# Two interleaved transformer layers on one core: the first loads, the bound check and the query weights rearranged

## The chip, the cores and the metric

The kernel runs on one core of a Trainium2 chip. Its metric is the device time of one execution in microseconds (us), from five runs. Five engines work side by side: TensorE (PE, with its weight loads shown apart as PEld), VectorE (DVE), ScalarE (ACT), GpSimd (POOL), and SyncE (SP), which issues most DMAs. Each engine takes its instructions strictly in its own order, and a wait holds up all that is behind it on that engine.

## The reference

The input x has 2048 rows of 576 bf16 values. Two kinds of block alternate, A, B, A, B, each added to x after a layer norm without scale or shift.

Block A is linear attention with 32 heads of width 18 and a learned feature map:

```
q, k, v  = split(ln(x) @ wqkv)                  # per head, width 18
pq, pk   = q @ w_phi, k @ w_phi                 # 18 x 18 per head
phi_q    = [softmax(pq), softmax(-pq)]          # 36 features, phi_k the same from pk
kv, z    = sum over rows of phi_k^T v, of phi_k
o        = (phi_q kv) / (phi_q z + 1e-6)
x        = x + o @ wo
```

Block B is a bilinear gated unit: x + ((ln(x) @ w_gate) * (ln(x) @ w_up)) @ w_down, with 4608 inner columns. Both layers use the same weights.

## The kernel before, in words

**Tiles.** The 2048 rows are 16 tiles of 128 rows (NS), handled in 8 pairs (NB). The kernel fuses w_phi into the query and key weights once: for each of five blocks `kt` of 128 rows of wqkv (the last has 64 rows) it turns the raw block (`Wraw`) by five PE transposes into `WT`, copies that out of PSUM, and multiplies it by a block diagonal form of w_phi (`BDphi5`) in two half-groups of three matmuls, each followed by a cast into `Wk` or `Wq` (`t_fuse1`). So a half-group is 16 heads of one block.

**A program in two versions.** If the fused projections can't overflow, exp needs no maximum. A bound is computed on the chip: PE multiplies every raw block by itself (`t_flag`, "Gram" matmuls, 10 for a block), DVE takes the maxima, three fp32 matmuls turn the columns of maxima, and four small DVE operations make a flag. All engines load the flag and branch to the fast or the general version of all that follows. What is recorded up to the mark is common to both versions and is called the shared part here. With these inputs the fast version runs.

**Layer 1, block A, after the branch.** For each tile: layer norm (`t_ln`: statistics on DVE, the affine step `xln` on DVE or POOL, then a transpose into `xT`, by PE for the first two pairs and by DMA on SP's queue for the others), value projection (`t_v`), key projection and its four exps on ACT (`fast_front`), row sums on DVE (L1327), reciprocals on ACT or DVE, two products on POOL (L1342), and the kv matmuls (`kv_ops`). For one tile a projection is 18 matmuls that use half the PE's rows each, two at a time. Key and value tiles stay in two PSUM banks of sums (`kvb`) until all 16 tiles are done; `t_barrier` then masks them into `BD`. Query projections (`t_qproj`) may start once tile 8 is accumulated (`pqg`), and are stored in the place of `xT`.

**From BD to block B.** Tiles 0 and 1 go through a chain of their own (`t_aout`: numerator, denominators, transposes, Wo, layer norm), and then block B starts on the first pair (`t_bmain`, `gu_quad`, L1662). It also waits for `wloaded`: the loads of Wr, Wg and Wu (10 MB) stand on SP behind the DMA transposes of the last pair of layer 1's layer norm, because part of that space holds `Wraw` and `WT` before.

**What sets the order.** Nothing is ordered by hand. Each piece of work is a thread of requests, and a planner (`Sched.run`) picks the request that could start first by its own duration estimates, shifted by priorities, by an `age`, and by a table of offsets for each thread (`AGES`). The choice between engines (`alt`) is made there too. The planned order of each engine is then the program, so a change of an estimate or of `AGES` moves instructions everywhere. SP issues x tile 0, raw blocks 0 and 2, x tile 1, raw block 4 as two halves of 64 partitions, the value weights and x pairs 1 to 3; ACT's queue issues w_phi and raw blocks 1 and 3 (`t_load`).

Of the kernel before, what the change touches and what calls it, by code (L numbers as in the profile page):

```python
# [19 lines left out]
    "ain1_10": -143, "ain1_12": -228, "ain1_13": 255, "ain1_14": 386, "ain1_5": -137, "ain1_9": -364, "ain2_14": -581, "aout1_0": 157,  # L20
    "aout1_2": -123, "aout1_3": -52, "aout2_0": -253, "aout2_1": 5, "aout2_2": -160, "aout2_3": -342, "bar1": -1385, "bar2": -651, "bdphi": 141,
    "bepi0": 843, "bepi6": 1283, "bepi7": -480, "fusek0": 115, "fusek1": 188, "fusek3": 103, "init": 18, "k2_6": -644, "k2ln0": 204, "k2ln1": 1008,
    "kv2_6": 13, "kv2_7": -60, "lnA1_0a": 99, "lnA1_0b": 308, "lnA1_1": 24, "lnA1_4": -54, "lnB1_0a": -834, "lnB1_0b": -218, "lnB2_0a": -48,
    "lnB2_0b": 270, "pq1_11": 192, "pq1_2": -84, "pq1_5": 108, "pq1_6": 202, "pq1_7": 20, "pq1_8": 114, "pq1_9": 166, "pq2_11": 158, "pq2_12": -146,
    "pq2_13": -162, "pq2_14": -2, "pq2_15": -156, "pq2_2": 116, "pq2_3": -76, "pq2_5": -209, "pq2_6": -46, "pq2_7": -103, "pq2_8": 448, "pq2_9": 459,
    "v1_0": -129, "v1_13": 57, "v1_14": -38, "v1_3": -2, "v1_4": 70, "v1_6": -13, "v1_8": -25, "v1_9": -41, "v2_14": -73, "v2_15": -358,
# [268 lines left out]
class Sched:  # L295
# [110 lines left out]
    def run(self):  # L406
        tr = self.tr
        while True:
            progressed = False
            again = True  # L410
            while again:
                again = False
                for th in list(self.threads):
                    while th.req is not None and th.req[0] not in ("ops", "alt", "pe2", "dma", "acq", "acqn"):
# [18 lines left out]
                        elif kind == "mark":  # L433
                            tr.set_mark(r[1])
                            t_ = self.tr.fin[tr.lastw[r[1]]] + 500.0
# [113 lines left out]
            else:  # L549
# [4 lines left out]
                start = max(issue, self.dma_free["sp"], 1300.0)  # L554
                xfer = nbytes / self.dma_bw
                self.dma_free["sp"] = start + xfer
                sp_time = r[8] if len(r) > 8 else 480.0
                fin = max(start + xfer + self.dma_lat, issue + 2.1 * sp_time) + (1500.0 if sp_time > 1000 else 0.0)
# [23 lines left out]
def d_pe(n):  # L582
    return max(n, 64) / 2.4 + (7.0 if 288 <= n < 512 else 3.0)
# [10 lines left out]
def d_actc(n):  # L594
    return n / 1.2 + 50.0
# [29 lines left out]
class K:  # L625
    def __init__(self, nc, A_x, A_wqkv, A_w_phi, A_wo, B_w_gate, B_w_up, B_w_down, out, fast, base=None):
# [10 lines left out]
        self.vlead = 5  # L637
        self.row2 = True
        self.fage = 300.0
        self.fageq = 0.0  # L640
        self.fage2 = 300.0
# [4 lines left out]
        self.qlead = 8 if fast else 8  # L646
# [3 lines left out]
        self.lnlead = 8  # L650
# [4 lines left out]
        self.pqg = 8 if fast else 10  # L655
# [21 lines left out]
    def alloc(self):  # L677
# [10 lines left out]
        self.cst = A("cst", [128, 4], F32)  # L688
        self.flg = A("flg", [1, 8], F32)
# [46 lines left out]
    def lend(self):  # L736
# [56 lines left out]
        self.sm_of = {}  # L793
        self.wd_slot = {}
# [3 lines left out]
        self.g_out = g("out")  # L798
        self.g_et = [g("et%d" % i) for i in range(self.NET)]
# [16 lines left out]
    def t_init(self):  # L816
# [19 lines left out]
            Op(100, lambda e: e.memset(s.mask9[:], 1.0), writes=[("mask9",)]),  # L836
            Op(100, lambda e: e.memset(s.maskf[:], 1.0), writes=[("maskf", 0), ("maskf", 1)]),
# [45 lines left out]
    def t_flag(self):  # L883
# [5 lines left out]
        gots = yield ("acqn", ["pb"], 2)  # L889
        banks = [g_[1] for g_ in gots]  # L890
        for kt in range(5):
            yield ("wait", ("ld", "raw", kt))
            yield ("ops", "pe", [Op(55, (lambda e, m=m, c0=c0, kt=kt, bank=banks[m // 3], c=128 * (m % 3), st=(kt == 0 and c0 == 0 and m in (0, 3)): e.matmul(
                s.ps[:, bank, c:c + 128], s.Wraw[:, kt, c0 + 128 * m:c0 + 128 * m + 128], s.Wraw[:, kt, c0 + 128 * m:c0 + 128 * m + 128], start=st, stop=(kt == 4 and c0 > 0), skip_group_check=True)),
                reads=[("Wraw", kt)], writes=[("pbd", banks[m // 3])], excl=[("pb", banks[m // 3])]) for c0 in (0, D) for m in range(5)])
        yield ("ops", "dve", [Op(d_dve(n), (lambda e, c=c, bank=bank, n=n: e.tensor_reduce(s.cst[:, c:c + 1], s.ps[:, bank, 0:n], AX.X, ALU.max)),
                                 reads=[("pbd", bank)], writes=[("cst", c)], excl=[("pb", bank)]) for c, bank, n in ((1, banks[0], 384), (2, banks[1], 256))])
        for bank in banks:
            yield ("rel", "pb", bank)
        (_, bank), = yield ("acqn", ["pb"], 1)  # L900
        yield ("ops", "pe", [Op(150, (lambda e, c=c: e.matmul(s.ps[0:1, bank, 128 * c:128 * c + 128], s.cst[:, c:c + 1], s.identf[:], start=(c == 0), stop=(c == 2), skip_group_check=True)),
                                reads=[("cst", c), ("identf",)], writes=[("pbd", bank)], excl=[("pb", bank)]) for c in range(3)])
# [3 lines left out]
        yield ("ops", "dve", [  # L906
            Op(470, (lambda e: e.tensor_reduce(s.flg[0:1, 0:3], s.ps[0:1, bank, 0:384].rearrange("p (c n) -> p c n", c=3), AX.X, ALU.max)), reads=[("pbd", bank)], writes=[("flg", 0)], excl=[("pb", bank)]),
            Op(70, (lambda e: e.tensor_tensor(s.flg[0:1, 3:4], s.flg[0:1, 1:2], s.flg[0:1, 2:3], ALU.max)), reads=[("flg", 0)], writes=[("flg", 1)]),
            Op(70, (lambda e: e.tensor_scalar(s.flg[0:1, 4:5], s.flg[0:1, 3:4], s.flg[0:1, 0:1], s.flg[0:1, 0:1], ALU.mult, ALU.mult)), reads=[("flg", 0), ("flg", 1)], writes=[("flg", 2)]),
            Op(70, (lambda e: e.tensor_scalar(s.flag[0:1, 0:1], s.flg[0:1, 4:5], lim, None, ALU.is_lt)), reads=[("flg", 2)], writes=[("flag",)])])  # L910
        yield ("rel", "pb", bank)
# [3 lines left out]
    def t_load(self):  # L915
# [15 lines left out]
        def rawload(kt, queues):  # L931
            n = 128 if kt < 4 else 64
            g = tr.dma_group("raw%d" % kt)
            for p, queue in zip(range(0, 128, n), queues):
                yield ("dma", g, (lambda e, p=p: e.dma_start(s.Wraw[p:p + n, kt, :], wqkv[128 * kt:128 * kt + n, 0:2 * D + 64])), (), [("Wraw", kt)], n * (2 * D + 64) * 2, False, False, 540.0, queue)
            yield ("dmaclose", g, queue)
            yield ("sig", ("ld", "raw", kt))

        def x0load(j):
            return grp("x0%d" % j, [((lambda e: e.dma_start(s.x_sb[:, j, :], xv[:, j, :])), [("x", j, c_) for c_ in range(2)], 128 * D * 2)], ("ld", "x0", j))  # L940
# [11 lines left out]
        def side():  # L952
            yield from grp("wphi5", items, ("ld", "wphi5"), "act")
            yield from rawload(1, ["act"])
            yield from rawload(3, ["act"])

        yield ("go", side(), 9, "side")
        yield from x0load(0)
        yield from rawload(0, ["sp"])
        yield from rawload(2, ["sp"])  # L960
        yield from x0load(1)
        yield from rawload(4, ["sp", "sp"])
        yield ("wait", "zeroed")
        yield from w5(s.Wv, wqkv[:, 2 * D:3 * D], "Wv", "wv")
        yield from xload(1)
        yield from xload(2)
        for b in range(3, NB):
            yield ("wait", ("xT", 1, b - 3))
            yield from xload(b)
            if b == 6:  # L970
                yield from w5(s.Wo, s.A_wo, "Wo", "wo")
# [31 lines left out]
    def t_fuse1(self, which, kt):  # L1003
# [6 lines left out]
        (_, bank), = yield ("acqn", ["pb"], 1)  # L1010
        P = s.psb16[bank]
        yield ("ops", "pe", [Op(60, (lambda e, k=k: e.transpose(P[:, 128 * k:128 * k + 128], s.Wraw[:, kt, c0 + 128 * k:c0 + 128 * k + 128], s.ident[:])),
                                reads=[("Wraw", kt), ("ident",)], writes=[("pbd", bank)], excl=[("pb", bank)]) for k in range(5)])
        wv, pv = WT[:, kt, :, :], P[:, 0:640].rearrange("p (k n) -> p k n", k=5)
        cp = [(lambda e, wv=wv, pv=pv: e.tensor_copy(wv, pv)), (lambda e, wv=wv, pv=pv: e.copy(wv, pv))]
        yield ("alt", [(eng, [Op(dur, em, reads=[("pbd", bank)], writes=[("WT", which, kt)] + [("WT", which, 5)] * (kt == 4), excl=[("pb", bank)])])
                       for eng, dur, em in (("act", d_actc(640), cp[1]), ("dve", 360, cp[0]))])
        yield ("rel", "pb", bank)
        for half in range(2):
            (_, bank), = yield ("acqn", ["pb"], 1)  # L1020
            ops = []
            for k in range(5):
                h0, h1 = max(7 * k, 16 * half), min(7 * k + GH, 16 * half + 16, H)
                if h0 < h1:
                    ops.append(Op(d_pe(DH * (h1 - h0)) + 25, (lambda e, k=k, a=h0 - 7 * k, b=h1 - 7 * k, c=DH * (h0 - 16 * half), c1=DH * (h1 - 16 * half), bank=bank, st=not ops: e.matmul(
                        s.ps[:, bank, c:c1], WT[:, kt, k, :], s.BDphi5[:, k, a:b, :], start=st, stop=True, skip_group_check=True)),
                        reads=[("WT", which, kt), ("BDphi5",)] + [("WT", which, 5)] * (kt == 4), writes=[("pbd", bank)], excl=[("pb", bank)]))
            yield ("ops", "pe", ops)
            r = slice(0, 128) if kt < 4 else slice(64 * half, 64 * half + 64)
# [12 lines left out]
    def t_ln(self, tiles, sig, fast=False, slot=None, banks=None):  # L1042
# [48 lines left out]
        for j in js:  # L1091
# [10 lines left out]
                           for eng, dur in (("pool", (620, 200)[:2 - fast]), ("dve", (400,) if fast else (400, 200)))[:1 + (fast or boot)]])  # L1102
# [168 lines left out]
    def t_qproj(self, L, st_):  # L1271
# [10 lines left out]
        for h in range(2):  # L1282
            bank = banks[h]
            yield ("ops", "act", [Op(d_actc(288), (lambda e, h=h, bank=bank: e.copy(s.pq(st_)[:, 288 * h:288 * h + 288], s.ps[:, bank, 0:288])),
# [741 lines left out]
```

## Time and profile before

| | |
|---|---|
| median of five runs | 1078.37 us (1075.63 to 1079.98) |
| profiled execution, its own time | 1074.55 us |
| its span, first to last instruction | 1072.8 us |
| PE, PEld, DVE, ACT, POOL busy | 98%, 75%, 45%, 32%, 19% |
| mean granted TensorE clock | 0.997 of full speed |
| first block B matmul of layer 1 (L1662) | 98.5 us after the start |
| first instructions after the branch | 17.4 us after the start |

The busy share of PE is not peak use, because the ends of pipelined matmuls are modelled. The shares are averages over a first stage of some 98 us, in which all engines take turns, and the rest, in which PE is hardly ever idle. The change acts in the first stage, so the views that count are those of its windows.

### The profile page before, as it was taken

How to read it: one execution, taken by the hardware profiler on the slowest of the kernel's cores; microseconds unless marked ns; L12 is line 12 of the kernel's file. 1: busy time of each engine (PE TensorE's matmuls, PEld its weight loads, DVE VectorE, ACT ScalarE, POOL GpSimd, SP SyncE). 2: the span in 40 equal slices, each digit the busy share in tenths (PEclk: the TensorE clock that was granted, in tenths of full speed). 3: DMA queues.
4: the chain of work that ended last, by engine and by line, in shares of the span. 5: the costliest groups of instructions: out<-in, count | busy, mean ns of one | idle time of the engine just before them, and what ended most of it. 6: DMA issues, size and time to landing. Idle time of an engine off the chain costs nothing.

```text
span 1072.8 us, 34304 instructions
## 1 busy us (share of the span) xinstructions
PE 1048.9 (98%) x15750; PEld 805.5 (75%) x15812; DVE 483.3 (45%) x974; ACT 346.1 (32%) x838; POOL 202.1 (19%) x232
## 2 busy tenths in 40 slices
PE   7999999999999999999999999999999999999997
PEld 5667868778686878878686786877778786868683
DVE  6985535354343525435242754434344343424131
ACT  5777223324141423314141742222313131302030
POOL 2874004031220403103120030201010101000000
PEclk9999999999999999999999999999999999999999
DMA  5495274361917346171606034536272719080704
GB/s 141 108 313 199 36 205 69 91 157 25 223 27 209 52 131 129 48 179 36 200 15 177 24 59 129 130 99 160 72 188 45 214 24 236 15 222 16 211 2 147
DMA packets 177642, 127.79 MB, mean 119 GB/s; under 512 B 96592, under 2 KB 175696, under 8 KB 176336
## 3 DMA queue, kind: packets, MB, share of 16 engines
q1 hardware_dynamic: 176592, 124.85, 45.1%
q8 instruction: 126, 2.06, 0.8%
q10 hardware_dynamic: 896, 0.64, 0.2%
q14 instruction: 28, 0.23, 0.1%
HBM read 100.82 MB, written 2.36 MB: 96 GB/s over the span
## 4 chain that ended last, share of the span: by engine, by line
PE 92%; DMA 2%; POOL 2%; DVE 2%; ACT 1%; issue 1%; ACTq 0%
PE ps L1662 53%; PE ps L1736 21%; PE ps L1140 11%; PE ps L1738 4%; PE ps L1523 1%; DMA wdx<-in_B_w_down_dram 1%; POOL dd_w3f L1342 1%; PE ps L1381 1%; PE ps L1128 1%; DVE xln L1099 1%; POOL dd_h1g L1342 1%; DMA Wraw<-in_A_wqkv_dram 0%; DVE ss_w4f L1327 0%; DMA wdr<-in_B_w_down_dram 0%; PE ps L1107 0%
## 5 line engine op out<-in xcount | busy, mean ns | idle before, releaser
L1662 PE MATMUL ps<-xT,Wg 64*128 64x256 bf16 x4608 | 582.2, 269 | 0.0
L1662 PE MATMUL ps<-xT,Wu 64*128 64x256 bf16 x4608 | 582.0, 269 | 0.0
L1662 PEld LDWEIGHTS ps<-xT,Wu 64*128 64x128 bf16 x4608 | 431.7, 94 | 27.6 <-DVE x_sb L1777 0.3
L1662 PEld LDWEIGHTS ps<-xT,Wg 64*128 64x128 bf16 x4608 | 430.3, 94 | 29.0 <-issue 3.1
L1711 DVE TENSOR_TENSOR hT<-ps,hT 128x512 bf16<-128x512 f32 x288 | 199.0, 691 | 300.0 <-ACT hT L1709 300.0
L1709 ACT CAST hT<-ps 128x512 bf16<-128x512 f32 x288 | 168.4, 585 | 412.8 <-PE ps L1662 402.8
L1736 PE MATMUL ps<-wdr,hT 128*128 128x512 bf16 x922 | 237.7, 380 | 0.1
L1738 PE MATMUL ps<-wdr,hT 128*128 128x64 bf16 x960 | 184.9, 193 | 2.3 <-issue 0.5
L1342 POOL TENSOR_TENSOR dd<-dd,ss 128x576 bf16<-128x576 bf16 x92 | 107.5, 1193 | 415.3 <-ACT ss L1338 415.2
L1736 PEld LDWEIGHTS ps<-wdr,hT 128*128 128x128 bf16 x960 | 93.9, 98 | 111.0 <-DMA wdr<-in_B_w_down_dram 0.4
L1662 PE MATMUL ps<-xT,Wr 64*128 64x256 bf16 x1152 | 170.1, 269 | 0.0
L1099 POOL TENSOR_SCALAR xln<-x_sb,nmean,rstd 128x64 bf16<-128x64 bf16 (+1 forms) x94 | 58.1, 624 | 340.6 <-DVE nmean L1080 158.5
L1779 DVE TENSOR_TENSOR x_sb<-ps,x_sb 128x64 bf16<-128x64 f32 x32 | 7.0, 219 | 223.5 <-PE ps L1738 223.5
L1738 PEld LDWEIGHTS ps<-wdr,hT 128*128 128x128 bf16 x960 | 94.1, 98 | 0.2
L1338 ACT ACTIVATE ss<-ss 128x64 f32<-128x64 f32 x92 | 23.6, 258 | 175.7 <-DVE ss L1327 174.8
L1327 DVE TENSOR_REDUCE ss<-dd 128x64 f32<-128x1152 bf16 x48 | 63.8, 1346 | 21.2 <-ACT dd L1261 16.1
L1662 PEld LDWEIGHTS ps<-xT,Wr 64*128 64x128 bf16 x1152 | 66.8, 94 | 6.3
L1140 PE MATMUL ps<-Wk,xT 64*128 64x288 bf16 x576 | 49.2, 283 | 2.3 <-ACT vx_w0g L1370 1.4
L1736 PE MATMUL ps<-wdx,hT 128*128 128x512 bf16 x168 | 50.4, 380 | 1.0 <-DMA wdx<-in_B_w_down_dram 1.0
L1140 PE MATMUL ps<-Wv,xT 64*128 64x288 bf16 x576 | 49.2, 289 | 0.0
L1066 DVE BATCH_NORM_STATS2 st<-x_sb 128x6 f32<-128x288 bf16 x120 | 46.3, 444 | 2.4 <-DMA x_sb<-in_A_x_dram 1.6
L1140 PE MATMUL ps<-Wo,oT 64*128 64x288 bf16 x504 | 40.4, 283 | 0.0
(120 smaller groups left out, 739.2 us busy)
## 6 DMA issues: line engine op xcount, KB each, us to landing
wdr<-in_B_w_down_dram SPq DMA_DIRECT2D x240, 288.0 KB, 3.7
wdx<-in_B_w_down_dram SPq DMA_DIRECT2D x48, 288.0 KB, 3.8
Wg<-in_B_w_gate_dram SPq DMA_DIRECT2D x4, 1152.0 KB, 14.7
Wu<-in_B_w_up_dram SPq DMA_DIRECT2D x4, 1152.0 KB, 16.8
out_dram<-x_sb SPq DMA_DIRECT2D x16, 144.0 KB, 2.5
x_sb<-in_A_x_dram SPq DMA_DIRECT2D x7, 288.0 KB, 4.2
xT<-xln SPq DMA_TRANSPOSE x54, 2.6
Wraw<-in_A_wqkv_dram SPq DMA_DIRECT2D x2, 304.0 KB, 3.9
```

Source lines behind the costliest of these rows:

```text
L1066: ops.append(Op(d_dve(288), (lambda e, j=j, h=h, src=src: e.bn_stats(st[:, sl[j], 6 * h:6 * h + 6], src)), reads=rd, writes=[("st", sl[j], ...
L1099: em = [(lambda e, j=j, a=a, b=b, c=c: e.tensor_scalar(xln[:, sl[j], a:b], x_sb[:, ss[j], c:c + b - a], s.nmean[:, sl[j]:sl[j] + 1], rstd[ ...
L1128: full = [Op(d_pe(N), (lambda e, k=k, h=h: e.matmul(s.ps[:, banks[h], 0:N], L[:, k, :], Wm[:, k, N * h:N * h + N], start=(k == 0 and fresh ...
L1140: out.append(Op(61, (lambda e, h=h, k=k, st=(i == 0 and k == 0), sp=(i == 1 and k == 3): e.matmul(s.ps[:, banks[h], 0:N], L[r, k, :], Wm[r ...
L1327: Op(1265, (lambda e: e.tensor_reduce(ss[:, sm, :], e4, AX.X, ALU.add)), reads=s.ddk(sm, 0) + s.ddk(sm, 1), writes=[("ss", sm)]),
L1338: yield ("ops", "act", [Op(200, (lambda e, kw=kw: e.activation(ss[:, sm, :], ss[:, sm, :], **kw)), reads=[("ss", sm)], writes=[("ss", sm)])])
L1342: yield ("alt", [(eng, [Op(dur, (lambda e, ev=ev, rb=rb: e.tensor_tensor(ev, ev, rb, ALU.mult)), reads=s.ddk(sm, br) + [("ss", sm)], write ...
L1662: out.append(Op(54.3, (lambda e, bank=bank, cs=cs, lhsT=lhsT, rhs=rhs, st=st, sp=sp: e.matmul(ps[:, bank, cs].rearrange("p (a n) -> p a n" ...
L1709: yield ("ops", "act", [Op(480, (lambda e, gb=gb, p=p: e.copy(hT[:, p, :], ps[:, gb, :])), reads=[("gu", gb)], writes=[("hT", p)] + (s.raw ...
L1711: yield ("ops", "dve", [Op(600, (lambda e, ub=ub, p=p: e.tensor_tensor(hT[:, p, :], ps[:, ub, :], hT[:, p, :], ALU.mult)), reads=[("gu", u ...
L1736: ops = [Op(d_pe(512), (lambda e: e.matmul(s.ps[:, bank, 0:512], lhsT, s.wslot(slot)[:, fi, 0:512], start=(f == 0), stop=(f == NF - 1))), ...
L1738: Op(d_pe(64) + 3, (lambda e: e.matmul(s.ps[:, z, 64 * sl:64 * sl + 64], lhsT, s.wslot(slot)[:, fi, 512:576], start=(f == 0 and (sl == 0 o ...
```

## The change

All edits are in what is done up to about 90 us; the table `AGES` and some estimates of the planner are replaced, which can move the order of later work too.

1. Loads: raw block 1 and x tile 1 now come first. SP issues x tile 1, raw 1, raw 2, x tile 0, raw 3, raw 4, the value weights, x pairs 1 to 3; ACT's queue issues w_phi and raw 0. The last raw block is read as rows 448 to 575, so it fills 128 partitions with one load, and its fusing uses the lower 64 columns for both halves.
2. The bound: the part that concerns w_phi is a chain of its own (`t_m2`), done early. At the end of the Gram matmuls (order 1, 0, 2, 4, 3) DVE compares the two maxima of each partition with the limit, PE counts the partitions that pass, and DVE compares the count with 255.5.
3. Query weights: the five PE transposes of a block and the copy are replaced by one DMA transpose on SP's queue.
4. Planner: value and query casts of layer 1 may go to DVE as well as ACT; value projections may run 9 tiles ahead instead of 5; query projections may start after tile 4 instead of 8; layer norms 10 tiles ahead instead of 8; the two kv banks are taken after the branch; new estimates for the branch, the first loads and the POOL layer norm step.

In the planned order that results, before the first block B matmul all 288 half-row query matmuls stand ahead (before: 190 of them and 20 full-row ones, 12.6 of 16 tiles). Three of ten key half-groups are fused ahead of the branch (before: eight). Ahead of the last layer norm step on DVE stand 14 row sums (before: 10). The block diagonal `BDphi5` is made on POOL (before: DVE).

```diff
@@ t_flag, and the new t_m2
+    def t_m2(self):
...
         yield ("ops", "dve", [Op(160, lambda e: e.tensor_reduce(s.cst[:, 0:1], s.wst5[:], AX.XY, ALU.max, apply_absolute_value=True), ...
+        yield ("ops", "pe", [Op(250, lambda e: e.matmul(row, s.cst[:, 0:1], s.identf[:], ...
+        yield ("ops", "dve", [Op(200, lambda e: e.tensor_reduce(s.flg[0:1, 0:1], row, AX.X, ALU.max), ...
+                              Op(150, lambda e: e.tensor_scalar(s.flg[0:1, 1:2], s.flg[0:1, 0:1], s.flg[0:1, 0:1], None, ALU.mult), ...
+        yield ("ops", "pe", [Op(250, lambda e: e.matmul(col, s.onesf[0:1, :], s.flg[0:1, 1:2], ...
+        yield ("ops", "dve", [Op(150, lambda e: e.tensor_copy(s.cst[:, 3:4], col), ...
...
+        yield ("wait", "m2")
+        yield ("ops", "dve", [Op(120, (lambda e: e.tensor_scalar(s.f01[:], s.cst[:, 1:3], s.cst[:, 3:4], lim, ALU.mult, ALU.is_lt)), ...
+        yield ("ops", "pe", [Op(60, (lambda e, c=c: e.matmul(n01, s.f01[:, c:c + 1], s.one16[:], ...
+        yield ("ops", "dve", [Op(150, (lambda e: e.tensor_scalar(s.flag[0:1, 0:1], n01, 255.5, None, ALU.is_gt)), ...
-        yield ("ops", "pe", [Op(150, (lambda e, c=c: e.matmul(s.ps[0:1, bank, 128 * c:128 * c + 128], s.cst[:, c:c + 1], s.identf[:], ...
-        yield ("ops", "dve", [
-            Op(470, (lambda e: e.tensor_reduce(s.flg[0:1, 0:3], ...
-            Op(70, (lambda e: e.tensor_tensor(s.flg[0:1, 3:4], ...
-            Op(70, (lambda e: e.tensor_scalar(s.flg[0:1, 4:5], ...
-            Op(70, (lambda e: e.tensor_scalar(s.flag[0:1, 0:1], ...
@@ t_load
+            r0 = 128 * kt if kt < 4 else D - 128
+            em = lambda e: e.dma_start(s.Wraw[:, kt, :], wqkv[r0:r0 + 128, 0:2 * D + 64])
...
+        self.sload = [['x0', 1], ['raw', 1], ['raw', 2], ['x0', 0], ['raw', 3], ['raw', 4], ['wv', 0], ['x', 1], ['x', 2], ['x', 3]]
+        self.aload = [['raw', 0]]
@@ t_fuse1
+        if which in s.wtdma:
+            yield ("dma", s.g_wt[kt], (lambda e: e.dma_start_transpose(WT[:, kt, :, :], s.Wraw[:, kt, c0:c0 + 640])), ...
@@ t_qproj (t_v the same)
-            yield ("ops", "act", [Op(d_actc(288), (lambda e, h=h, bank=bank: e.copy(s.pq(st_)[:, 288 * h:288 * h + 288], s.ps[:, bank, 0:288])),
+            yield ("alt", [(eng, [Op(dur, em, reads=[("pbd", bank)], writes=[("xT", st_)], excl=[("pb", bank)])]) for eng, dur, em in (
+                ("act", d_actc(288), (lambda e, h=h, bank=bank: e.copy(...))),
+                ("dve", d_dve(288), (lambda e, h=h, bank=bank: e.tensor_copy(...))))[:1 + (L == 1 and s.qalt)]])
@@ settings
-        self.vlead = 5
+        self.vlead = 9
-        self.lnlead = 8
+        self.lnlead = 10
-        self.pqg = 8 if fast else 10
+        self.pqg = 4 if fast else 10
@@ t_layer1
-        gots = yield ("acqn", ["pb"], 2)
-        s.kvb = [g_[1] for g_ in gots]
...
         yield ("wait", "branch")
+        gots = yield ("acqn", ["pb"], 2)
+        s.kvb = [g_[1] for g_ in gots]
```

## The prediction

> **What bounds the kernel now.** The granted clock is full over the span, so I ask first where PE stands idle. The windows answer that (columns: length; busy us and instructions of PE, PEld, DVE, ACT, POOL; granted clock; DMA share; GB/s):
>
> ```profile
> 17.39:33.47 16.08, 15.54 (x196) 10.10 (x197) 14.19 (x32) 12.25 (x41) 6.38 (x9) 0.89 0.30 69
> 33.47:52.70 19.23, 17.81 (x270) 12.67 (x269) 18.45 (x39) 14.28 (x52) 16.37 (x17) 1.00 0.51 110
> 52.70:65.64 12.94, 11.50 (x168) 7.67 (x166) 10.70 (x18) 10.15 (x34) 8.81 (x9) 1.00 0.85 167
> 65.64:79.74 14.10, 13.77 (x211) 10.35 (x210) 12.15 (x13) 10.63 (x35) 10.23 (x10) 1.00 1.02 423
> ...
> 98.40:540.00 441.60, 440.02 (x6742) 345.70 (x6766) 196.91 (x406) 135.21 (x324) 96.19 (x110) 1.00 0.46 112
> ```
>
> From 98.4 us on PE works 99.6% of the time: what PE has to do there is only moved by when it begins. Between 33 and 53 DVE (96%) is as full as PE. So the change is worth what it takes from the first 98.4 us. Second, the chain of waits of the start, and the clock after it:
>
> ```profile
> 12.03 0.56 PE ps L893 x10
> 12.59 0.28 PE ps L1012 x5
> 12.87 0.19 PE ps L1025 x3
> ...
> 14.69 0.76 PE ps L901 x6
> ...
> 15.47 0.56 DVE flg L907
> ...
> 16.53 0.15 DVE flag L910
> 16.68 0.72 issue
> 17.40 0.31 PE ps L1025 x3
> ```
>
> ```profile
> 14.16:17.58 3.42, 1.70 (x20) 1.08 (x19) 1.98 (x7) 1.52 (x4) 0.22 (x1) 1.00 0.00 0
> 17.58:20.99 3.41, 3.41 (x31) 2.02 (x30) 3.28 (x13) 1.65 (x4) 0.66 (x4) 0.52 0.00 0
> ```
>
> PE stands still for 1.9 us while DVE makes the flag and the engines branch, and the next 3.4 us run at half clock. Third, the timeline and the landings of the DMAs issued near 66 us, for what block B waits for:
>
> ```profile
> 59.35 2.54 SPq L1114 DMA_TRANSPOSE xT<-xln  x2
> 61.93 0.58 SPq L977 DMA_DIRECT2D Wg<-in_B_w_gate_dram  x1
> 98.51 0.27 PE L1662 MATMUL ps<-xT,Wg 64*128 64x256 bf16 x1
> ```
>
> ```profile
> Wu<-in_B_w_up_dram SPq DMA_DIRECT2D x1, 1152.0 KB, 23.6
> ```
>
> The weight loads start when the last pair's transposes are issued, and the last of them, issued at 66.0, lands at 89.6: 27.7 us after the first was issued and 8.8 us before block B begins. This slack is the number to watch.
>
> **The branch.** The landings of the first DMAs before were 4.5 (second on SP), 6.2 and 7.5 (third, fourth), 7.2 (first block on ACT's queue), 8.7 and 10.0 (the last two blocks). The same slots and nearly the same bytes give 4.5 for raw 1, 6.2 raw 2, 7.2 raw 0, 7.5 x tile 0, 8.7 raw 3, 10.0 raw 4. The last block's 128 partitions cost nothing, since two halves of 64 moved as many bytes. On PE ten Gram matmuls take 1.07 us slow and 0.56 fast (two rows of the chain; it turns fast near 10.8). Gram 1 ends at 5.6; the transposes of x tile 1 (0.67) and the new w_phi chain fit before raw 0 lands at 7.2; their cover is PE's old wait there of 0.8, and without it they would cost PE up to 0.8. Gram 0 and 2 end at 9.35, fifteen key transposes (0.55 per five) at 11.0, then 0.28 + 0.19 + 20 Gram matmuls 1.12 = 12.6. DVE's two maxima (0.89) and the compare (0.15, as L910) end at 13.8, the count on PE at 14.0 (two one-column matmuls, under the 0.76 of the six passes they replace). A copy of 0.49 stands ahead of the flag on DVE: 14.35; flag 0.15, branch 0.72: 15.2. `BDphi5` on POOL takes some 1.5 (1.19 for 576 elements) from 4.8 to 6.3 and is wanted at 11.3: hidden; without that cover the first fuse would wait. Ends: 14.7 if the copy has passed, 17.4 (as before) if raw 4 lands 2 us later. I take 15.2: 2.2 earlier.
>
> **What follows the branch.** Five more half-groups of the key fuse stand behind it: 5 x 0.19 = 0.95 on PE, and 5 x 0.40 = 2.0 of casts on ACT ahead of the first key projection, which so begins near 20.4 (before 21.45). At least 0.95 is lost, at most 2.0.
>
> **The clock.** The window that was throttled after was half idle (1.70 of 3.42 busy). The new stop is about 1.6 us less the count, so a window stays at least some 55% busy: just above. The nearest row is throttled, so I take no gain; the other end is 31 matmuls at full clock, 1.6 us. The Trainium skill (TensorE: Matmul & The Clock Gate, Part 1) would halve the clock only after an idle window of about 3.4 us; by it neither the old stop nor the new one should be punished. The row above contradicts it for the old stop. By the page the sum would not change, by a threshold at one half it would be 1.6 us better at most.
>
> **Query weights by DMA.** PE loses 25 transposes, 4 x 0.28 + 0.55 = 1.7 us; DVE loses 3 copies of 0.47, ACT 2 of 0.73. SP gets five DMA transposes: issue 2.54 / 2 = 1.27 each, 2.6 to landing. Behind them on SP stand the x loads and xT transposes; SP waits for `xln` most of this stage, which hides 6.4 us of issue. Without that cover each would delay a pair by 1.3 us, and the fuse matmul that needs it would hold up PE by up to 2.6.
>
> **Query projections moved ahead.** 12.6 tiles stood before block B, now 16: 62 half-row matmuls of 0.0605 (36 take 2.38 less the last one's tail), 3.75 us of PE work that leaves the 99.6% stage. Block B at 98.4 + 3.75 = 102.15 would be no change; that is the mark to compare with.
>
> **When can block B begin?** Two paths end there.
> PE: from the branch to BD before took 63.4 us (17.4 to 80.8, where `BD` begins). Its issue work by the counts of the plan: 576 key and value matmuls at 0.0605, 36 half-row and 20 full-row query ones (0.0605, 0.122), 144 kv at 0.039 (18 take 0.86 less a tail of 0.16), 36 of the fuse at 0.06, 55 transposes at 0.056: 50. The change adds 8.5 query tiles (18 x 0.0605 = 1.09 each, 9.3) and 0.95, less 1.7: 58.6. At the 91% of the 65.6 to 79.7 window (12.9 us of issue in 14.1) BD stands at 79.6; at 95% at 77; at the old BD's place at most a little later, 83. From BD on, the old stretch of 17.6 held 134 query matmuls between the chain's links; now 62. The links by their rows (masks 1.0, numerators 0.54, denominators 0.7, division 0.95, transposes 0.57, copy 0.70, Wo 1.39, casts 0.83, statistics 1.4, scale 0.9, transposes and copy 1.1), plus the second tile's 3 us, make 13.2. So 90 to 96.
> Loads: DVE's work from the branch to the last `xln` was 42.6 by group means (the trace: 42.0). Now 4 row sums of 1.34, 6 value and 2 query casts near 0.43 (cast of Wq, 0.437) and one `xln` 0.66 are ahead of it, 3 copies of 0.47 gone: +8.0, 50.6. So 15.2 + 50.6 = 65.8 if DVE sets the pace. If the projections set it, it comes after the fourteenth row sum, which ended at 68.5 before: 68.5 - 2.2 + 2.8 = 69.1. I take the middle, 67.5, as nothing tells which. Two transposes 2.5, then 27.7: **97.7**, between 96.0 and 99.3. The loads are later than PE's path, so they are what is late next.
>
> **The sum.** 102.15 - 97.7 = 4.45, so span 1068.4, profiled execution 1070.1. Layer 2 and the end are counted as unchanged: PE idles about 0.6 us between 540 and 600 around the layer change, which bounds a gain from the new offsets; a loss there is not excluded, and I allow 1.5. The median stands 3.8 above the profiled time; I assume the same: 1078.37 - 4.4 = **1074.0**.
>
> **Rivals.**
> A. The start is faster but it is spent again: the branch at 16.5, raw 4 late, and the loads at their late end, 99.3 + 1.3 = 100.6. Gain 1.5, 1076.9. For it: DVE is full from 33 to 53 and its post-branch work up to BD rises from 56.2 to about 58.4. Against it: the gaps of DVE between 60 and 80 (3.8 us).
> B. Slower: the weight loads. It is decided at a last `xln` of 67.5 + 102.15 - 97.7 = 72.0; beyond that every microsecond is lost one for one. If query projections, which share six free PSUM banks and ACT with keys and values, spread the row sums so that the fourteenth ends at 75, `xln` ends at 77.8 and block B begins at 108: 5.9 slower, 1084; at 72 + 3.3 it is 0.3% slower. For it: two query tiles now stand right in front of the ninth key tile, and all sixteen end before BD's chain does. Against it: the pace of PE before, 75% up to 65, leaves room.
> C. All goes well: clock kept (1.6) and DVE pace (1.7), the PE path at its early end: 94.5, gain 7.7, 1070.7.
> D. The change doesn't take the transposes off the path: PE waits for WTq instead, 5 x 2.6 = 13 at most; half of it, 6.5, turns the gain of 4.45 into a loss of 2.05, 1080.4. Against it: SP issues the first at the branch and PE wants it near 22, after six us of issue work; for it: PE wants the last three within 1.5 us of issue work of each other, and SP issues them 1.27 apart.
>
> **How the numbers follow.** Forecast 0.42 (its own range 1071.5 to 1075.8), A 0.25, B 0.12, C 0.13, D 0.08. About 0.3% (3.2 us) is what a measurement of this kernel can tell from no change. Faster by more: most of the forecast (0.40), all of C, a little of A: 0.55. Slower by more: B, a third of D, and 0.02 for the layer change: 0.17. Within: 0.28. The range leaves out B's end and the best of C: 1069.5 to 1080.0.
>
> **What would show it.** The first instruction after the branch near 15.2; DVE's last `xln` of the stage at 66 to 69; the last Wu landing near 96 to 97, with block B's first matmul behind it; the granted clock after the branch at half or not; no wait of PE for WTq over 1 us. The prediction is wrong if the last `xln` ends past 72, or if PE is idle for long between BD and block B while the weights have landed, or if the offsets open gaps of PE at the layer change.

## The result, and the profile after

The changed kernel takes 1080.58 us (median of 31 runs, 1078.34 to 1083.46), the kernel before beside it 1077.57 (52 runs). The ratio is 1.0027 (95% interval 1.0020 to 1.0035): slower by 3.0 us, where 1074.0 was forecast. The profiled execution has a span of 1080.9 us and a time of 1082.62.

The windows of the changed kernel, cut at the branch, at three groups of kv matmuls, at `BD` and at the first gate matmul of block B (columns: length; busy us and instructions of PE, PEld, DVE, ACT, POOL; granted clock; DMA share; GB/s):

```profile
15.84:32.34 16.50, 15.23 (x211) 9.95 (x212) 14.09 (x37) 13.76 (x47) 8.69 (x13) 1.00 0.73 129
32.34:50.65 18.31, 16.09 (x251) 11.69 (x251) 16.20 (x37) 13.79 (x48) 14.16 (x14) 1.00 0.47 90
50.65:66.25 15.60, 15.34 (x244) 11.44 (x242) 10.95 (x15) 12.29 (x40) 9.84 (x9) 1.00 0.61 99
66.25:92.90 26.65, 22.53 (x314) 14.41 (x314) 13.42 (x18) 14.74 (x45) 9.59 (x8) 1.00 0.72 281
92.90:107.45 14.55, 12.39 (x146) 7.49 (x143) 11.98 (x24) 11.37 (x31) 4.72 (x4) 1.00 1.00 313
107.45:540.00 432.55, 429.36 (x6522) 337.74 (x6552) 192.27 (x399) 129.15 (x307) 91.73 (x104) 1.00 0.46 112
```

The fourth window is the loss. It is 26.65 us long, and in it DVE works half the time and PE leaves 4.1 us idle. On average no engine is full there, but the average hides two halves: DVE first stands still twice, for 4.14 and 7.90 us, and then works without a pause. The timeline of the changed kernel shows the order behind this (start us, us, engine, line, operation, tiles, count, and in brackets the idle time before it and its releaser):

```profile
51.43 0.27 DVE L1119 BATCH_NORM_AGGREGATE mv<-st 128x2 f32<-128x12 f32 x2
66.76 0.19 ACT L1128 ACTIVATE nmean<-mv 128x2 f32<-128x2 f32 x1
70.41 0.46 DVE L1331 CAST xT<-ps 128x288 bf16<-128x288 f32 x1 [4.14 <-ACT xT L1330]
70.78 1.43 DVE L1144 TENSOR_SCALAR xln<-x_sb,nmean,rstd 128x576 bf16<-128x576 bf16 x4
71.57 2.53 SPq L1159 DMA_TRANSPOSE xT<-xln  x2
73.86 4.75 PE L1185 MATMUL ps<-Wq,xT 64*128 64x288 bf16 x62
74.15 0.58 SPq L1018 DMA_DIRECT2D Wg<-in_B_w_gate_dram  x1
78.92 0.29 PE L1185 MATMUL ps<-Wk,xT 64*128 64x288 bf16 x1 [0.32 <-ACT dd L1306]
80.11 2.61 DVE L1373 TENSOR_REDUCE ss<-dd 128x64 f32<-128x1152 bf16 x2 [7.90 <-ACT dd L1306]
107.45 0.27 PE L1715 MATMUL ps<-xT,Wg 64*128 64x256 bf16 x1 [0.90 <-ACT xT L1155]
```

The statistics of the last pair are ready at 51.7 (first row). The next step of that layer norm, a small one on ACT, comes at 66.76, 15 us later. Its scale step on DVE (the last `xln`) stands behind a query cast, for which DVE waits 4.14 us. Meanwhile PE works through query projections, ten tiles in all ahead of the last pair's first key projection at 78.92, and DVE then waits another 7.90 us for that pair's exps. From there to just before `BD` DVE is the engine that is full, 0.99 busy with the row sums, reciprocals, products and casts that have come late all at once (window of the changed kernel):

```profile
80.10:91.88 11.78, 8.89 (x116) 5.45 (x115) 11.67 (x12) 6.42 (x21) 5.64 (x4) 1.00 1.01 425
```

`BD` follows at 92.9 (before 80.8) and block B at 107.45 (before 98.51).

The chain of the start in the changed kernel, and the clock windows around its first gate matmul:

```profile
12.46 1.03 PE ps L931 x18
...
13.51 0.90 DVE cst L934 x2
...
14.44 0.23 DVE f L940
14.67 0.39 DVE WTk L1060
15.06 0.07 DVE flag L944
15.12 0.71 issue
15.84 1.21 PE ps L1071 x15
```

```profile
104.17:107.59 3.42, 1.88 (x24) 1.14 (x26) 3.02 (x8) 2.90 (x7) 1.26 (x2) 1.00 0.60 110
107.59:111.00 3.41, 3.41 (x36) 2.94 (x34) 2.05 (x4) 1.79 (x5) 2.33 (x2) 0.50 0.18 40
```

The short chain does what it should: the branch is over at 15.84 instead of 17.40. The half-clock stretch behind it is gone, but another one has come at the beginning of block B, behind a window in which PE was 0.55 busy.

Each kernel was profiled a second time. In stages (borders: PE's first instruction after the branch, then gate matmuls 0, 2048, 2304 and the last of 4608; us, first profile / second):

| stage | before | changed |
|---|---|---|
| start to branch | 17.40 / 18.66 | 15.84 / 16.52 |
| branch to gate 0 | 81.11 / 81.14 | 91.61 / 91.65 |
| gate 0 to 2048 | 435.12 / 435.27 | 434.50 / 433.96 |
| gate 2048 to 2304 (layer change) | 82.79 / 83.57 | 85.74 / 83.78 |
| gate 2304 to the last | 430.76 / 430.60 | 428.85 / 429.80 |
| last gate to the end | 25.62 / 25.67 | 24.33 / 24.28 |
| span | 1072.8 / 1074.9 | 1080.9 / 1080.0 |

The stage from the branch to block B repeats within 0.04 us, so its length belongs to the program and not to the single execution. It is 10.5 longer; 3.75 of that is query work that the next stage no longer has, so **6.75 us are lost there**. The second profiles differ by 5.1 us in span, the first by 8.1, the medians by 3.0. The rest between 5.1 and 3.0 is not explained by these profiles.

### The profile page after: what moved, and what is told of

Read it like the earlier page. It is cut to its first block, busy times and chain, and to the rows that moved or that the text cites. A ratio compares the mean times of both kernels' runs of the same rounds, so it can differ in the third digit from the quotient of the medians.

```text
span 1080.9 us, 34298 instructions
## 1 busy us (share of the span) xinstructions
PE 1051.3 (97%) x15741; PEld 806.8 (75%) x15803; DVE 479.2 (44%) x976; ACT 345.6 (32%) x837; POOL 199.6 (18%) x230
## 4 chain that ended last, share of the span: by engine, by line
PE 93%; DMA 2%; ACT 2%; DVE 2%; issue 1%; ACTq 0%
PE ps L1715 52%; PE ps L1789 21%; PE ps L1185 12%; PE ps L1791 4%; PE ps L1575 1%; DMA wdr<-in_B_w_down_dram 1%; PE ps L1427 1%; DMA Wraw<-in_A_wqkv_dram 1%; DMA wdx<-in_B_w_down_dram 1%; PE ps L1173 0%; PE ps L1152 0%; ACT dd_h1g L1306 0%; DVE ss_w4f L1373 0%; DVE dd_h1g L1388 0%; PE ps L931 0%
## 5 line engine op out<-in xcount | busy, mean ns | idle before, releaser
L1144 POOL TENSOR_SCALAR xln<-x_sb,nmean,rstd 128x576 bf16<-128x576 bf16 x90 | 54.4, 611 | 267.2 <-DVE nmean L1125 181.6
L1185 PE MATMUL ps<-Wq,xT 64*128 64x288 bf16 x576 | 43.3, 284 | 4.8 <-DVE vx_h2g L1417 1.9
## 6 DMA issues: line engine op xcount, KB each, us to landing
Wg<-in_B_w_gate_dram SPq DMA_DIRECT2D x4, 1152.0 KB, 13.5
```

What stands on the lines that cost most here:

```text
L1144: em = [(lambda e, j=j, a=a, b=b, c=c: e.tensor_scalar(xln[:, sl[j], a:b], x_sb[:, ss[j], c:c + b - a], s.nmean[:, sl[j]:sl[j] + 1], rstd[ ...
L1185: out.append(Op(61, (lambda e, h=h, k=k, st=(i == 0 and k == 0), sp=(i == 1 and k == 3): e.matmul(s.ps[:, banks[h], 0:N], L[r, k, :], Wm[r ...
```

## The experiments

The table has, for every kernel run, the end of the last `xln`, the start of `BD`, the stage from the branch to gate 0, the query tiles that stand ahead of block B, that stage at equal query work (18 half-row matmuls of 0.0605 us, 1.09 a tile, taken off or put on to 12.6 tiles), and the ratio to the kernel before with its interval.

| kernel | last xln | BD | stage | tiles | at 12.6 tiles | ratio |
|---|---|---|---|---|---|---|
| before | 59.4 | 80.8 | 81.1 | 12.6 | 81.1 | 1 |
| changed | 72.2 | 92.9 | 91.6 | 16 | 87.9 | 1.0027 (1.0020 to 1.0035) |
| 1 last pair's offset zero | 53.2 | 80.7 | 81.2 | 10.6 | 83.4 | 0.9992 (0.9981 to 1.0004) |
| 2 queries after tile 8 | 52.9 | 81.9 | 82.8 | 10 | 85.6 | 1.0014 (1.0001 to 1.0027) |
| 3 changed, no offsets | 60.3 | 92.7 | 91.6 | 16 | 87.8 | 1.0089 (1.0068 to 1.0110) |
| 4 before, no offsets | 69.1 | 86.3 | 83.6 | 14 | 82.1 | 1.0053 (1.0035 to 1.0072) |
| 5 loads and bound alone | 61.1 | 84.0 | 84.1 | 12.6 | 84.1 | 1.0005 (0.9991 to 1.0018) |
| 6 and query weights by DMA | 59.2 | 85.0 | 85.8 | 12.6 | 85.8 | 1.0019 (1.0008 to 1.0029) |
| 9 before, stop filled | 59.6 | 81.0 | 79.8 | 12.6 | 79.8 | 0.9979 (0.9969 to 0.9989) |
| 10 offsets fitted anew | 56.6 | 83.0 | 81.6 | 16 | 77.9 | 0.9912 (0.9898 to 0.9926) |

**Theories.** "Order": the edits are sound, and the loss comes from query projections and casts that stand ahead of the last pair's chain to `BD`. Its rivals: the added casts fill DVE and ACT ("work"), the gain is given back at the layer change, or the edits at the start cost.

### 1 and 2. One number, and another number that should do the same

```diff
 AGES (of the changed kernel)
-    "lnA1_7": -410,
```

> The changed kernel with one number of the offsets set to zero: the layer norm of the last pair is no longer put back by 410. In the order that results 72 half-row query matmuls (4 tiles) stand ahead of the last pair's first key projection, in the changed kernel 180 (10 tiles), before none; 190 stand ahead of block B (before 190 and 20 full-row ones, changed 288). Against the kernel before, no change would be a first gate matmul at 98.5 - 2.4 = 96.1. Theory 'order' (the last pair stands behind the query projections, its scale step sets BD and BD sets block B): last scale step (xln) between 50 and 60 instead of 72.2, BD between 75 and 82 instead of 92.9, first gate matmul 14.5 to 17.6 behind BD, so at 91 to 98; median 1073 to 1078. Rival 'work' (the added casts of DVE and ACT fill the stage, whatever the order): BD at 88 or later although the last xln is early, gate at 102 or later, median 1079 or more. Rival 'given back': gate at 91 to 98, but the layer change takes the gain again, median 1079 or more.

The median is 1076.21, 4.4 below the changed kernel and level with the kernel before. In the timeline of this kernel the scale steps of the last four tiles run in one go and end at 53.2, and `BD` comes 12.3 us earlier, though the edits are the same:

```profile
50.42 2.74 DVE L1144 TENSOR_SCALAR xln<-x_sb,nmean,rstd 128x576 bf16<-128x576 bf16 x8
80.65 1.01 DVE L1518 TENSOR_TENSOR BD<-ps,maskf 128x380 bf16<-128x380 f32 x2 [0.44 <-PE ps L1427]
```

All casts are still on the engines that the change allows, so "work" falls. The layer change took 83.89 here (83.78 in the second profile of the changed kernel), so "given back" falls too. At equal query work 4.5 of the 6.75 us are back. Of the 2.3 that remain, up to 1.7 can be a half-clock stretch of 3.41 us that begins at 80.9, behind a window in which PE was 0.36 busy.

```diff
-        self.pqg = 4 if fast else 10
+        self.pqg = 8 if fast else 10
```

> The changed kernel with query projections allowed from tile 8 on, as before the change, instead of tile 4; the offset of the last pair stays. 36 half-row query matmuls stand ahead of the last pair's first key projection, 180 ahead of block B; no change against before would be a first gate matmul at about 95.5. Theory 'order': the last pair's steps have no query casts to stand behind, so this repairs the same thing by another hand: last xln between 50 and 60, BD between 75 and 84, gate at 91 to 99, median 1073 to 1079, within 2 us of the run with the offset at zero. If the offset itself were the cause, whatever stands around it: last xln at 68 or later again and a median of 1079 or more. Rival 'work': BD at 88 or later.

With the offset of -410 still there, the last `xln` ends at 52.9. So the offset does harm only together with the early query projections. By the planner's rule it lets whatever could start up to 410 ns later go first; that with query casts about there always was something is an inference from these two runs. The median, 1079.14, lies 2.9 above the first run, not within 2 as I had expected, and just above the 1079 of the forecast for it. The stage is 2.2 longer at equal query work, with a wait of 3.4 us for the transposes of a pair and a half-clock stretch behind it at 49.4.

### 3 and 4. Both kernels without offsets

```diff
-AGES = {
-    "ain1_0": 172, "ain1_1": 799, "ain1_10": 98, ...
-}
+AGES = {}
```

> The changed kernel with an empty table of offsets, to be compared with the kernel before with an empty table: so the edits are priced without a table that was fitted to either. If the edits are worth what the rows say (branch 1.6 earlier, no half-clock stretch after it 1.6, query transposes 1.7): 2 to 5 us below the kernel before with an empty table. If the edits themselves (casts on DVE, transposes on SP) are what costs: equal to it or above it. Against the kernel before with its own table I expect both to be slower, 1080 to 1092, as the order is not fitted.

> The kernel before with an empty table of offsets. If the table carries the order of the first stage, the last xln comes later than 59.4 and BD later than 80.8, and the median is 1082 to 1093. If the table is worth little: 1077 to 1080.

I had expected the edits to win 2 to 5 us; they lost 3.8 (1087.01 against 1083.24). The last `xln` is early in the third kernel (60.3), and yet `BD` is at 92.7. Its timeline shows the same fault in another place:

```profile
82.48 1.43 DVE L1378 TENSOR_TENSOR dd_h1g<-dd_h1g,ss_w4f 128x576 bf16<-128x576 bf16 x2
81.97 10.24 PE L1175 MATMUL ps<-Wq,xT 64*128 64x288 bf16 x162
92.14 0.87 PE L1417 MATMUL ps<-vx_h2g,dd_h1g 128*128 128x76 bf16 x18
```

The last products are done at 83.9, but their kv matmuls stand behind nine query tiles (162 matmuls, 9.8 us) and run at 92.1. So it isn't the last `xln` as such: query projections, which nobody needs until after block B has begun, may stand anywhere in front of the chain to `BD`.

### 5 and 6. The start alone, then the turned query weights, with the order held

Here the planner follows the order and the engines of the kernel before behind the branch, as far as the requests are the same.

```diff
 (on the changed kernel; its loads, t_m2, t_flag stay; other settings and AGES as before)
-        self.vlead = 9
+        self.vlead = 5
-        self.wtdma = 'q'
+        self.wtdma = ''
-        self.pqg = 4 if fast else 10
+        self.pqg = 8 if fast else 10
...
+            if self.held is not None and hasattr(self, "mark_time"):
+                best = self.follow(best)
```

> The kernel before with the new loads and the new chain of the bound alone (and the kv banks taken after the branch). Everything behind the branch keeps the order and the engines of the kernel before, except that seven key half-groups instead of two stand first there, as in the changed kernel. By the rows of the changed kernel the branch ends near 15.8 instead of 17.4, so 1.6 earlier; five half-groups cost PE 0.95 and ACT 2.0 of it. Theory 'order' (this part is worth little either way, the loss of the changed kernel lies in the order behind it): first gate matmul at 96.5 to 99, median 1075.5 to 1078.5. If the half-clock stretch of 3.4 us goes with the shorter stop: 1.6 better, at the low end. Rival 'the first part costs': gate at 100 or later, median 1079 or more.

The time is that of the kernel before (1.0005), as "order" had it, but the first gate matmul came at 101.7, where I had put the rival (100 or later). The branch gained nothing here: the flag was there at 16.5, and the first fuse behind it waited for a cast on ACT until 17.63. The stage grew by 3.0 us. Of that up to 1.7, by my estimate, is a second half-clock stretch (3.41 us at half speed), in the windows of this kernel:

```profile
57.68:61.09 3.41, 1.96 (x26) 1.09 (x24) 3.35 (x9) 2.21 (x9) 1.32 (x2) 1.00 0.77 175
61.09:64.50 3.41, 3.41 (x32) 2.15 (x30) 2.11 (x3) 2.46 (x10) 2.34 (x3) 0.50 1.00 212
```

The same wait of 1.4 us stands at 56.8 in the kernel before, and its window from 55.3 (1.97 of 3.41 busy, where run 5 has 1.96) went unpunished. I put the rest, 1.3 or somewhat more, down to the five key half-groups behind the branch; no run has them alone.

```diff
-        self.wtdma = ''
+        self.wtdma = 'q'
```

> As the run with the loads and the bound alone, and the five query weight blocks are turned by DMA on SP, each issued right behind the half-group before it; the order is held otherwise. PE loses 1.7 us of transposes, DVE 1.4 and ACT 1.5 of copies before BD; SP gets five issues of 1.27 ahead of layer norm transposes. Theory 'order': 0 to 2 us better than the run without it, no wait of PE for the turned weights over 1 us, gate 0 to 2 earlier. Rival D of the prediction (PE waits for the turned weights, or a pair's transposes come late behind them): gate later by 1 to 6.5 us, and the wait shows on the fuse matmul (L1071 in the changed kernel) or on a projection behind a transpose of xln.

Nothing was won; the median is 0.6 above the run without it. Rival D of the prediction is what happened, at its small end: the first gate matmul came 1.0 later than in run 5. The first line is from the waits of PE in this kernel (us in all, times, longest), the others from its timeline:

```profile
PE ps L1127 <- DMA WTq<-Wraw: 3.2, 1, 3.2
```

```profile
59.16 1.20 SPq L1215 DMA_TRANSPOSE xT<-xln  x1
60.40 1.28 SPq L1108 DMA_TRANSPOSE WTq<-Wraw  x1
```

The last block's transpose stood on SP behind one that had to wait for `xln`, and landed 5.5 us after it was issued, at 65.9. PE had come to it at 62.7. In the changed kernel the same DMAs cost PE no wait: in its order the last of them was issued at 39.6, not behind a wait for a late `xln`, and landed at 42.1, and PE came to it at 43.95.

### 7 and 8. Both kernels again

> The kernel before once more, for a second profile. The first profiled execution was 3 us quicker than the median of its runs, so if that comes from waits that differ between executions, this one shows more of them: span 1073 to 1078, the same order, first gate matmul at 98 to 99.5, and waits of PE for the down weights (wdr, wdx) between 0.5 and 4 us in all instead of 1.0. If the span repeats within 1 us, the gap to the median is not in the span.

> The changed kernel once more, for a second profile: last xln at 72 +- 0.5, BD at 92 to 93.5, first gate matmul at 106.5 to 108, as the order sets them; the waits of PE for wdr and wdx, 3.4 us in the first profile, between 0.5 and 4, and the span between 1077 and 1081 accordingly.

The orders repeat: the distances from the branch to block B are those of the first profiles. Some of the times that I had expected, counted from the span's start, are missed by up to 0.4 us (gate 0 at 99.8 and 108.2, the last `xln` at 72.9, `BD` at 93.6), as the branch came 1.3 and 0.7 later. Of the 2.1 us by which the two profiles of the kernel before differ, 1.26 is the branch: the last raw block landed at 9.91 in one execution and at 11.25 in the other, from the same issues. The waits for down weights in the changed kernel (3.4 in the first profile) are 1.6 in the second.

### 9. The price of the half-clock stretch

```diff
+        yield ("ops", "pe", [Op(40, (lambda e: e.matmul(s.ps[:, banks[1], 0:512], s.ident[:], s.Wraw[:, 0, 0:512], ...)) for _ in range(5)])
```

> The kernel before with five more matmuls of 512 columns on PE, written to a bank that nobody reads, between the matmuls that turn the maxima and the branch; the order behind the branch is held but for one key half-group, which now stands behind it. They fill about 1.1 of the 1.7 us that PE stands still there, so the window ahead of the stretch at half clock (0.50 busy in both profiles of before) is 0.8 busy. In all profiles so far a window of 3.41 us that was 0.57 busy or less is followed by 3.41 us at half clock, with two exceptions of 0.58, and one that was 0.61 or more is not. Theory 'half-idle window': no half-clock stretch behind the branch, branch to first gate matmul 79 to 80.2 instead of 81.1 in both profiles of before (1.7 gained, up to 0.4 given back for the half-group), median 1 to 1.7 us below the kernel before. Rival 'the branch itself throttles': the stretch stays and the time is equal within 0.5 us.

The stretch is gone (windows of this kernel; the branch ends in the second):

```profile
13.25:16.66 3.41, 3.41 (x56) 3.04 (x54) 2.19 (x5) 3.27 (x9) 0.00 (x0) 1.00 0.24 79
16.66:20.07 3.41, 2.63 (x24) 1.13 (x21) 2.28 (x8) 1.11 (x3) 0.88 (x4) 1.00 0.00 0
20.07:23.49 3.42, 3.37 (x55) 2.52 (x54) 2.99 (x13) 2.57 (x10) 0.25 (x1) 1.00 0.00 0
```

The stage is 1.3 us shorter and the time 0.2% (0.9979, 0.9969 to 0.9989), by matmuls whose result nobody reads. The 0.2% are 2.3 us, more than the stage shows; within its interval (1.2 to 3.3 us) the 1.3 fits. This is the cleanest of the gains, and it needs none of the change.

### 10. The changed kernel with its offsets fitted anew

```diff
-    "ain1_0": 172, "ain1_1": 799, "ain1_10": 98, "ain1_11": -16, ...
+    "ain1_0": 83, "ain1_1": -5, "ain1_10": -72, "ain1_11": -138, ...
```

> The changed kernel with the table of offsets fitted anew to it, nothing else changed. All 288 half-row query matmuls stand ahead of block B, as in the changed kernel (no change against before would be a first gate matmul at 102.15), but 126 instead of 180 of them ahead of the last pair's first key projection. Theory 'order' (the edits were held back by the order that the offsets made): last xln at 50 to 62, BD at 80 to 87, first gate matmul at 96 to 101, median 1071 to 1075.5, below both kernels. Rival 'the edits are worth nothing': 1077 to 1079. Rival 'given back': gate at 101 or less, but the layer change 1 to 3 us longer than before and the median at 1076 or more.

The median is 1068.12 (four runs), 0.88% below the kernel before (9.3 us) and 12.5 below the changed one: better than the best end that I had expected. Two windows of this kernel, the one that ends at `BD` and the next, answer to the fourth and fifth of the changed one:

```profile
66.90:83.02 16.12, 15.20 (x260) 11.87 (x260) 14.20 (x17) 12.16 (x36) 13.13 (x11) 1.00 1.02 427
83.02:98.43 15.41, 14.60 (x193) 9.70 (x190) 12.13 (x29) 12.10 (x32) 4.65 (x4) 1.00 0.74 254
```

All 16 query tiles stand ahead of block B and it begins at 98.4, 3.7 ahead of the mark of 102.15; so it is not the number of tiles ahead that costs, but where they stand. From 13.5 us to the last 3.2 us nothing runs at half clock. So with another order the same edits are faster than both kernels. About 3.2 of the 9.3 us stand in the stage at equal query work (81.1 against 77.9). How much of the 9.3 belongs to the edits and how much to the fitting stays open: neither the kernel before with a table fitted in the same way nor the fitted kernel with its query weights turned by PE was measured.

## Why the prediction was wrong, point by point

1. **The branch: right, smaller.** 1.6 (17.40 to 15.84) and 2.1 in the second pair of profiles (with the later landing in the kernel before), forecast 2.2. Raw 0 landed at 7.99, not 7.2, and twenty key transposes, not fifteen, came next.
2. **Five half-groups behind the branch: not contradicted.** About 1.3 is left for them in run 5, forecast 0.95 to 2.0.
3. **The clock: the sum was right by accident.** The forecast kept the stretch behind the branch. It went away, and one at block B came in its place (both profiles). Its price, bounded at 1.6 from above, was 1.3 in run 9, with one half-group more behind the branch there.
4. **Query weights by DMA.** In the changed kernel PE did not wait for them, as forecast. In run 6 rival D came true with 3.2 us. That the 1.7 us of PE transposes are a gain is shown by no run.
5. **Moved query work: right.** From gate 0 to 2048 the changed kernel is 1.3 shorter in the second pair: 3.75 moved away, 1.7 of half clock and 0.8 of a wait for down weights came.
6. **The start of block B: the step that failed.** Forecast 97.7, measured 107.45. The wrong path is the one to `BD`: put at 79.6, at most 83, measured 92.9. Three things in the step were wrong.
   - The last `xln` at 67.5 was the middle of two bounds, the work of DVE and the pace of the row sums. It ended at 72.2, with DVE idle for 4.1 us before the cast that stands right ahead of it. The order of the changed kernel showed ten query tiles ahead of the last pair's first key projection and query casts ahead of its scale step. I counted tiles as work and row sums in front, not what stood in front of the one chain that mattered. The work of DVE was misread as well: the 42.0 us that I took for it in the trace of before is the whole length from the branch to that `xln`, of which DVE was busy for 39.25. In the changed kernel DVE was busy for 43.0 us of that stretch, not 50.6, and idle for another 13.4, for which the sum had no term.
   - `BD` "at 79.6, at most 83" came from the PE's issue work at an efficiency. But `BD` ends a chain that begins with that `xln`, and the trace of before had its length, 21.4 us from the end of the step to `BD` (rows below). In the changed kernel it was 20.7. The forecast's own 67.5 plus 21.4 is 88.9, and with its 13.2 to block B (measured 14.6) it makes 102.1: no change. That 20.7 lies so near to 21.4 is luck, for other orders gave from 17.2 (run 4) to 32.4 (run 3). But even the shortest of them puts `BD` at 84.7 in the forecast and at 89.4 for the measured 72.2, past the 83 that was given as the most.
   - The weight loads were named as what is late next. They were issued 12 us later, but had landed by 100.4, 26.3 after the first issue (forecast 27.7), and block B waited 7 us more for the chain from `BD`.

The rows for this: DVE's timeline of the kernel before for the second point, and SP's timeline and the DMA list of the changed kernel for the third (issue at 77.95, landing 22.5 us later).

```profile
58.63 0.76 DVE L1099 TENSOR_SCALAR xln<-x_sb,nmean,rstd 128x576 bf16<-128x576 bf16 x2
80.83 1.01 DVE L1466 TENSOR_TENSOR BD<-ps,maskf 128x380 bf16<-128x380 f32 x2 [0.44 <-PE ps L1381]
```

```profile
77.95 0.74 SPq L1019 DMA_DIRECT2D Wu<-in_B_w_up_dram  x1
Wu<-in_B_w_up_dram SPq DMA_DIRECT2D x1, 1152.0 KB, 22.5
```

7. **The rest, counted as unchanged.** The layer change differed by 0.2 in the second pair; the 2.95 of the first holds one wait of 1.8 us for down weights. The end became 1.3 shorter, which no step foresaw.
8. **From the profile to the median.** The forecast took the median to lie 3.8 above the profiled time, as before. In the changed kernel it lies 2.0 below. By the spans the forecast missed by 12.5 us (1068.4 against 1080.9), by the medians by 6.6: half of the miss was hidden by chance.

Of the rivals, B had the right place and the right side, for a wrong reason: not the loads but the chain to `BD` was late. That the last `xln` ended just beyond B's threshold of 72.0 is luck: by B's own rule 72.2 loses 0.2 us, and block B was 5.3 behind the mark.

## What to carry to other kernels

An edit to a planned kernel is also a new order, and the order can outweigh the edit: the same edits measured 1.0027 with one table and 0.9912 with another. So follow in the new order the one chain that ends last, ask on each engine what work that nobody awaits stands in front of its steps, and set its steps beside the old trace. A sum of busy times only bounds from below, and a distance along the chain in one trace is no constant either: from the last `xln` to `BD` it was 17.2 to 32.4 us in these kernels. To price an edit, hold the order and change the edit alone.

## What the runs showed of the hardware

- **A half-idle window is enough to halve the clock.** In twelve profiles cut into windows of 3.41 us, from the first stretch at full clock to 130 us, all twelve windows in which PE was 0.57 busy or less were followed by one at half clock, none of 0.61 or more was, and of six between 0.58 and 0.60 one was. The stretch lasts one window, so it costs up to 1.7 us by estimate (half of 3.41); filling the stop gained 1.3 in the stage of run 9. The Trainium skill (TensorE: Matmul & The Clock Gate, Part 1) has the window, 3413 ns on a grid of its own, which fits; it speaks of an idle window as the cause, and the rows here, which decide, show up to 0.57 busy ahead of a half-clock stretch. So a wait costs more or less by where it falls on the grid: PE's wait of 1.7 us at the branch of the kernel before lay in one window (0.50 busy) and was punished, one of 1.93 us that ended at 88.4 in the changed kernel lay across two (0.64 and 0.61) and was not. The wait of 1.4 us that run 5 and the kernel before share, punished in the one and not in the other, is another case: both windows were all but equally busy (0.57 and 0.58), at the very limit.
- **The landing of the first loads differs** from one execution to the next with the same issues: the last raw block came at 9.91 and 11.25 in the two profiles of the kernel before, at 10.35 and 11.54 in runs 4 and 9. The branch moves with it (17.40 and 18.66).
- **A DMA transpose of a 128 by 640 block took 2.5 to 5.6 us to land** (ten of them in the changed kernel and run 6), not the 2.6 of the forecast. The three slowest (5.4 to 5.6) were issued behind loads: one right behind Wo, one right behind x tiles, one behind Wr and a transpose. In the second profile of the changed kernel the one behind Wo took 6.5.
